# The last tail tile turned into token order and stored as plain rows, two late VectorE steps on ScalarE, and a new order of the last four pairs

## The chip, the cores and the metric

The kernel runs on one core of one Trainium2 chip. The metric is the device time of one execution in microseconds (us), from 3 runs; lower is better. A core has five engines with a queue each, which work side by side and wait for one another through semaphores: TensorE (PE: matrix products, with weight loads listed as PEld), VectorE (DVE), ScalarE (ACT), GpSimd (POOL) and SyncE (SP, used here to issue DMAs). ScalarE's queue issues a few DMAs too (ACTq in the profile). 16 DMA engines move the data.

## The reference

Attention with a relative position bias over 8 batches, 8 heads, 576 tokens and 64 values a head, and then a mixture of 8 rank-16 adapters on the 4608 rows of 512 columns that attention gives:

```python
scores = scale * np.matmul(q, k.transpose(0, 1, 3, 2)) + bias.transpose(2, 0, 1)[None, :, :, :]
attn = np.exp(scores - np.max(scores, axis=-1, keepdims=True))
attn = attn / (np.sum(attn, axis=-1, keepdims=True) + 1e-09)
x = (attn @ v).transpose(0, 2, 1, 3).reshape(B * S, H * D)
...
logits = x @ w_gate
topk = np.argpartition(-logits, K, axis=1)[:, :K]          # K = 2
w = np.exp(sel)                                             # the two logits, less the larger
w /= w.sum(-1, keepdims=True) + 1e-09
...
        z = x[mask] @ A[e]                                  # rows that chose adapter e in place k
        delta[mask] += w[mask, k, None] * (z @ B[e])
return (x + delta).astype(np.float32)
```

The bias depends on the distance of two tokens alone and is constant from distance 128 on.

## The kernel before

The work goes in 32 units, called pairs here: batch b and a pair of heads hp, `u = 4*b + hp`. The 576 tokens of a batch are 512 main tokens and a tail of 64. Main tokens are held in a strided order: partition p and block c hold token 4p + c, so a tile of 128 rows t (0 to 3) is the tokens 4p + t. Tails are held in the same manner, 16c + p for token 4p + c, and the tails of two batches share one tile of 128 rows (`xe`): batch 6 in rows 0 to 63, batch 7 in rows 64 to 127.

Each pair has the steps that one letter or two name in a table (`ORDER`, line 41), and `step` (line 838) carries them out. The table writes by hand the order in which every engine gets its instructions; an engine takes them in that order, and nothing reorders them later. The steps that matter here:

- `K0` to `K3`: scores of four blocks of keys on TensorE, then the exponential on ScalarE (lines 409 to 428; in the last pair `keys_part`, line 385, where K0 and K1 make the first half of the queries, K2 and K3 the second). The score tiles rotate through 3 buffers.
- `E`, `C`: edge and corner scores of the tails. `T`, `t`: transposes for a later pair and their copies on VectorE.
- `A`, `B` and `a`, `b`: products with the values on TensorE, and their normalisation on VectorE, both for the pair before.
- `Z z G W w V y D d S`: the adapters of a finished batch: gate logits and low-rank products, their gating on GpSimd and ScalarE, transposes, the product with `B` (`D`, a tile `dl`), the addition of x (`d`, `moe_add`, line 597) and the store (`S`). For the last two tiles of batch 6, x is added by four identity products on TensorE (line 805), and ScalarE copies the result.
- `l*`, `c*`: loads (issued on SP) and casts (on GpSimd).

In the last pair come the steps of the last group, the five tiles of batch 7 and the shared tail, in three parts: part 0 is tiles 0 and 1, part 1 tiles 2 and 3, part 2 tile 4 (the tail). `F01` and `F2` transpose the columns of the first three head pairs ahead of time (`last_x`, line 668); then `va`/`vb` (values), `norm`, `turn` and `copy` (transposes of the last columns and their copy), `za`/`zb` (logits and low-rank products), `ga` (top two, mask, tanh), `gb` (weights), `gt`/`gc` (transpose and copy), `delta` (product with `B`, line 801), `out` (output copy or addition) and `store`, each with its part or tile number and, at the end, the letter of its engine. Tile 4's output (`fol`) is stored in two halves, one from SP and one from ScalarE, in the form 4x16x512, four blocks of 16 rows: it brings the rows back into token order on the way to memory (`store_tail`, line 613). All output rows are 512 floats, 2 KB.

PSUM buffers: the pool `mm` has two that rotate among products, transposes and adapter tiles; at the end the banks of the scores become single tiles (`banks`, line 42).

Of the kernel before, what the change touches and what calls it, by code (L numbers as in the profile page):

```python
# [12 lines left out]
BF16 = mybir.dt.bfloat16  # L13
ALU = mybir.AluOpType
ACT = mybir.ActivationFunctionType
# [16 lines left out]
def _dram(t, offset, dims):  # L32
# [30 lines left out]
 'fin': '',  # L63
# [18 lines left out]
def kernel(  # L82
# [11 lines left out]
    nc = tc.nc  # L94
    B, H, S, D = q.shape
    NB = bias_table.shape[0]
    Dm = H * D
    E = moe_w_gate.shape[1]
    r = moe_A.shape[2]
    ER = E * r  # L100
    ZW = ER + E
    HP = H // 2
    scale = 1.0 / float(np.sqrt(D))
    inv = float(np.sqrt(D))
    FAR = 128
    SM = 512
# [7 lines left out]
    cp = ctx.enter_context(tc.tile_pool(name="const", bufs=1))  # L114
# [17 lines left out]
    half = [slice(0, 64), slice(64, 128)]  # L132
# [95 lines left out]
    for o in range(2):  # L228
        nc.vector.tensor_scalar(ones[NB * o:NB * o + NB, :GL - 33], bk[:, 32 * o:32 * o + GL - 33], row, None,
                                op0=ALU.is_equal)  # L230
    ident = cp.tile([128, 128], BF16, tag="ident")
# [48 lines left out]
    def select():  # L280
        nc.gpsimd.memset(sel, 0.0)
        nc.gpsimd.affine_select(out=sel, in_=sel, compare_op=ALU.not_equal, fill=1.0, base=-4,
                                pattern=[[1, 4 + Dm]], channel_multiplier=-4)

    AW = cp.tile([128, 4, ZW], BF16, tag="AW")
    Bc = cp.tile([ER, Dm], BF16, tag="Bc")
    A4f = cp.tile([128, E, 4, r], FP32, tag="A4f")
# [1 line left out]
    Bf = cp.tile([ER, Dm], FP32, tag="Bf")  # L289
    A4 = cp.tile([128, 4, ZW], BF16, tag="A4")  # L290
    sel = cp.tile([128, 4 + Dm], BF16, tag="sel")

    def weights_load():
        nc.sync.dma_start(out=A4f.rearrange("p e c r -> p e (c r)"),
# [296 lines left out]

    def moe_d(gr, t):
        dl = mp.tile([128, Dm], FP32, name="dl", tag="mm")
        delta(dl, gr.zT[t], gr.xT[t] if gr.last and t >= 2 else None)
        pending_d.append((gr, t, dl))

    def moe_add():
        gr, t, dl = pending_d.pop(0)
        ot = ms.tile([128, Dm], FP32, name="ot", tag="ot", bufs=4)
        if gr.last and t >= 2:  # L600
            nc.scalar.copy(ot, dl)
        else:
            nc.vector.tensor_tensor(ot, dl, gr.x[t], op=ALU.add)  # L603
        pending_s.append((gr, t, ot))
# [5 lines left out]
    def store_main(b, t, ot, eng=nc.sync):  # L610
        eng.dma_start(out=out[b * S:b * S + SM, :].rearrange("(p c) n -> p c n", c=4)[:, t, :], in_=ot)

    def store_tail(b, ot, engs=(nc.sync, nc.sync)):
        for o in range(2):
            engs[o].dma_start(out=out[(b + o) * S + SM:(b + o + 1) * S, :].rearrange("(p c) n -> c p n", c=4),
                              in_=ot[64 * o:64 * o + 64, :])


# [46 lines left out]
    fxs = cp.tile([128, HP * 640], BF16, tag="fx")  # L665
    fx = [fxs[:, i * 640:(i + 1) * 640].rearrange("p (n t) -> p n t", n=5) for i in range(HP)]

    def last_x(hps):
        x = [xs[B - 1][:, t, :] for t in range(4)] + [xe[(B - 1) // 2]]
        if len(hps) == 1:  # L670
            ps = mp.tile([128, 512], FP32, name="fx_ps", tag="mm")[:, :320]
        else:
            ps = score_tile("fx")[:, :, :320]
        for i, hp in enumerate(hps):
            w = (ps if len(hps) == 1 else ps[:, i, :]).bitcast(BF16).rearrange("p (n t) -> p n t", n=5)
            for t in range(5):
                nc.tensor.transpose(w[:, t, :], x[t][:, hp * 128:(hp + 1) * 128], ident)
        nc.vector.tensor_copy(fxs[:, hps[0] * 640:hps[0] * 640 + len(hps) * 640].rearrange("p (n t) -> p n t", n=len(hps)),
                              ps.bitcast(BF16) if len(hps) > 1 else ps.bitcast(BF16).rearrange("p (n t) -> p n t", n=1))

    fps = []

# [62 lines left out]
    def f_turn(g):  # L745
        w = take(f"t{g}")[:, :64 * len(parts[g])].bitcast(BF16).rearrange("p (n t) -> p n t", t=128)
        for i, t in enumerate(parts[g]):
            nc.tensor.transpose(w[:, i, :], x[t][:, xo:], ident)
        ps[f"t{g}"] = w

    def copier(eng):
# [12 lines left out]
                nc.tensor.matmul(fz[g]["z"][:, i, :], lhsT=fx[c][:, t, :], rhs=AW[:, c, :],  # L764
                                 start=(i == 0 and c == 0), stop=(c == 3), skip_group_check=True)

    def f_gate_a(g):
        l, n, z = fz[g], len(parts[g]), fz[g]["z"]
        top, ns, l["th"], l["mk"] = small(g, "top", 8), small(g, "ns", 1), small(g, "th"), small(g, "mk")
        for i in range(n):  # L770
            nc.vector.max(top[:, i, :], z[:, i, ER:])
        nc.vector.scalar_tensor_tensor(out=ns, in0=top[:, :, 0:1], scalar=-1.0,
                                       in1=top[:, :, 1:2], op0=ALU.mult, op1=ALU.subtract)
        nc.vector.tensor_tensor(l["mk"], z[:, :, ER:], top[:, :, 1:2].to_broadcast((128, n, E)),
                                op=ALU.is_ge)
        for i in range(n):
            nc.scalar.activation(l["th"][:, i, :], z[:, i, ER:], ACT.Tanh, scale=2.0, bias=ns[:, i, :])

    def f_gate_b(g):
        l, n, z = fz[g], len(parts[g]), fz[g]["z"]  # L780
        gate = small(g, "gate")
        nc.vector.scalar_tensor_tensor(out=gate, in0=l["th"], scalar=1.0, in1=l["mk"], op0=ALU.add,
                                       op1=ALU.mult)
        l["zt"] = ms.tile([128, n, E, r], BF16, name="fzt", tag=f"fzt{g}")
        nc.vector.scalar_tensor_tensor(out=l["zt"],
                                       in0=z[:, :, :ER].rearrange("p n (e r) -> p n e r", e=E),
                                       scalar=0.5, in1=gate.to_broadcast((128, n, E, r)),
                                       op0=ALU.mult, op1=ALU.mult)

    def f_gate_t(g):  # L790
# [10 lines left out]
    def delta(dl, zT, xT=None):  # L801
        nc.tensor.matmul(dl, lhsT=zT, rhs=Bc, start=True, stop=xT is None, skip_group_check=True)  # L802
        if xT is not None:
            for c in range(4):
                nc.tensor.matmul(dl[:, c * 128:(c + 1) * 128], lhsT=xT(c), rhs=ident,
                                 start=False, stop=(c == 3), skip_group_check=True)
# [4 lines left out]

    def f_out(t, eng):
        if t == 4:
            fz["ol"] = ms.tile([128, Dm], FP32, name="fol", tag="fol")
            o = fz["ol"]
        else:
            o = fot[t // 2][:, t % 2, :]
        if eng == "a":
            nc.scalar.copy(o, ps[f"d{t}"])
        else:  # L820
            nc.vector.tensor_tensor(o, ps[f"d{t}"], x[t], op=ALU.add)

    def f_store(t, eng):
        if t == 4:
            store_tail(B - 2, fz["ol"], (nc.sync, nc.scalar))
        else:
            engs[eng].dma_start(out=rows4[:, t, :], in_=fot[t // 2][:, t % 2, :])

# [155 lines left out]
```

## Time and profile before

| | |
|---|---|
| median of 3 runs | 193.26 us (193.12 to 193.83) |
| profiled execution | 191.99 us |
| its span, first to last instruction | 190.2 us |
| TensorE busy | 175.5 us (92%) |
| ScalarE busy | 162.2 us (85%) |
| VectorE busy | 142.7 us (75%) |
| GpSimd busy | 95.4 us (50%) |
| DMA | 39.25 MB, mean 206 GB/s |

Times within a profile are counted from the start of its span. Busy time is the sum of an engine's instructions; TensorE's ends are modelled, so its figure is no measure of how near its peak it is. In rows of a timeline the columns are start, duration, engine, line, operation, what is written and read, its count, and in brackets the idle time before it with what ended it.

### The profile page before, as it was taken

The page shows a single profiled execution, that of the slowest core. Times are in us where ns is not written, and L with a number is a line of the kernel's source. Part 1 is how long each engine was busy: PE and PEld are TensorE (multiplying, and loading weights), DVE is VectorE, ACT ScalarE, POOL GpSimd, SP SyncE. Part 2 cuts the span into 40 slices and gives each one's busy share as a digit, 9 for nine tenths or more (in the row PEclk, how much of TensorE's full clock was granted, in tenths as well). Part 3 has the DMA queues.
Part 4 walks back from the last instruction along what each step waited for, and adds up shares of the span by engine and source line. Part 5 has one row for each costly group of instructions (what it writes and reads, how often), then busy time and mean ns, then how long its engine had stood idle before and what let it go on. Part 6 is the DMA issues. An engine that isn't in the chain of part 4 may idle for free.

```text
span 190.2 us, 9407 instructions
## 1 busy us (share of the span) xinstructions
PE 175.5 (92%) x4028; PEld 124.8 (66%) x4028; DVE 142.7 (75%) x436; ACT 162.2 (85%) x192; POOL 95.4 (50%) x220
## 2 busy tenths in 40 slices
PE   6489999999999999999999999999999999999830
PEld 2245767787578777786678766876778667679510
DVE  4665666786788887889798788889788879777930
ACT  3089999989999999999998999999999999897620
POOL 7456838516961379336921597527703780720000
PEclk9999999999999999999999999999999999999996
DMA  4998799987978896989488997789697931113444
GB/s 159 237 267 240 205 252 275 295 179 199 274 230 184 263 257 188 248 246 276 126 241 175 299 264 229 182 264 262 161 245 174 319 109 59 59 59 104 163 143 146
DMA packets 71193, 39.25 MB, mean 206 GB/s; under 512 B 49520, under 2 KB 66416, under 8 KB 71152
## 3 DMA queue, kind: packets, MB, share of 16 engines
q1 hardware_dynamic: 70548, 37.96, 73.1%
q8 instruction: 31, 0.51, 1.2%
q10 hardware_dynamic: 604, 0.70, 1.1%
q14 instruction: 10, 0.08, 0.1%
HBM read 28.85 MB, written 9.44 MB: 201 GB/s over the span
## 4 chain that ended last, share of the span: by engine, by line
PE 70%; DMA 10%; SPq 6%; POOL 4%; ACT 2%; DVE 2%; issue 2%; ACTq 0%; POOLq 0%
PE sc L418 14%; PE pv L456 14%; PE tx L323 6%; PE sc L423 6%; PE dl L802 4%; DMA vs<-in_v_dram 4%; PE zl L536 4%; PE pv L475 4%; PE se L445 4%; DMA qkt<-in_k_dram 3%; PE pv L465 3%; SPq L153 3%; DMA A4f<-in_moe_A_dram 3%; SPq L156 2%; PE se L436 2%
## 5 line engine op out<-in xcount | busy, mean ns | idle before, releaser
L428 ACT ACTIVATE pk<-sc 128x1024 bf16<-128x1024 f32 x124 | 120.1, 1034 | 12.8 <-PE sc L423 12.6
L418 PE MATMUL sc<-qkT 64*64 64x512 bf16 x496 | 48.3, 397 | 1.6 <-DVE qkT L355 1.3
L456 PE MATMUL pv<-v,pk 128*128 128x65 bf16 x992 | 42.1, 194 | 0.0
L456 PEld LDWEIGHTS <-pk 128*128 128x128 bf16 x1024 | 38.1, 98 | 5.2 <-issue 3.5
L423 PE MATMUL sc<-Wt,anti 64*64 64x320 bf16 (+2 forms) x496 | 37.4, 279 | 0.1
L451 ACT ACTIVATE pt<-se 128x1024 bf16<-128x1024 f32 x32 | 33.4, 1045 | 1.8 <-PE se L447 0.9
L418 PEld LDWEIGHTS <-qkT 64*64 64x64 bf16 x496 | 15.8, 105 | 19.0 <-issue 5.4
L510 DVE TENSOR_TENSOR xn<-pv,rc 128x256 bf16<-128x256 f32 x62 | 26.3, 425 | 2.1
L360 DVE COPY qkT<-tx 128x512 bf16<-128x512 bf16 x32 | 22.0, 688 | 4.4 <-PE tx L323 3.9
L178 POOL CAST v<-vs 128x512 bf16<-128x512 f32 x32 | 19.8, 619 | 5.5 <-PE pv L456 2.8
L355 DVE COPY qkT<-tx 128x512 bf16<-128x512 bf16 (+2 forms) x32 | 21.5, 672 | 0.0
L603 DVE TENSOR_TENSOR ot<-dl,xn 128x512 f32<-128x512 f32 x26 | 17.5, 686 | 3.7 <-PE dl L802 3.7
L182 POOL CAST kn<-ks 128x512 bf16<-128x512 f32 x30 | 18.2, 611 | 3.2 <-DMA ks<-in_k_dram 3.0
L182 POOL CAST qn<-qs 128x512 bf16<-128x512 f32 x30 | 18.3, 610 | 1.8 <-DMA qs<-in_q_dram 1.5
L190 POOL CAST qkb<-qkt 128x512 bf16<-128x512 f32 x8 | 4.9, 611 | 27.9 <-DMA qkt<-in_k_dram 27.9
L509 DVE RECIPROCAL rc<-pv 128x4 f32<-128x4 f32 (+1 forms) x62 | 11.4, 184 | 9.2 <-PE pv L475 6.7
L465 PE MATMUL pv<-vc,pt 128*128 128x130 bf16 x124 | 17.0, 219 | 0.0
L423 PEld LDWEIGHTS <-anti 64*64 64x64 bf16 x496 | 15.6, 108 | 0.8 <-issue 0.6
L479 DVE TENSOR_TENSOR xe<-pv,rc 64x64 bf16<-64x64 f32 x62 | 13.6, 219 | 0.6
L547 DVE COPY z<-zl 128x272 f32<-128x272 f32 (+1 forms) x17 | 7.0, 414 | 7.9 <-PE zl L536 7.9
L445 PE MATMUL se<-qkT,tl 128*128 128x256 bf16 x64 | 12.8, 282 | 0.0
L323 PEld LDWEIGHTS <-kn 64*128 64x128 bf16 x256 | 6.0, 96 | 9.8 <-issue 3.4
(140 smaller groups left out, 293.2 us busy)
## 6 DMA issues: line engine op xcount, KB each, us to landing
qs<-in_q_dram SPq DMA_DIRECT2D x32, 256.0 KB, 3.3
vs<-in_v_dram SPq DMA_DIRECT2D x64, 128.0 KB, 4.7
ks<-in_k_dram SPq DMA_DIRECT2D x31, 256.0 KB, 4.1
out_dram<-ot SPq DMA_DIRECT2D x28, 256.0 KB, 5.5
qkt<-in_q_dram SPq DMA_DIRECT2D x8, 128.0 KB, 4.2
vt<-in_v_dram SPq DMA_DIRECT2D x16, 64.0 KB, 4.1
qkt<-in_k_dram SPq DMA_DIRECT2D x8, 128.0 KB
out_dram<-ot SPq DMA_DIRECT2D x6, 128.0 KB
```

What stands on the lines that cost most here:

```text
L178: eng.tensor_copy(t[:, :, :, :D].rearrange("p c h d -> p h c d"), s)
L182: copy(t.rearrange("p c h d -> p h c d"), s)
L355: nc.vector.tensor_copy(sb[:, k0:k1].rearrange("p k (g i) -> p g k i", g=2), ps[:, :, k0 * 64:k1 * 64].rearrange("p g (k i) -> p g k i", i ...
L360: nc.vector.tensor_copy(sb[:, 0:4].rearrange("p k j -> p (k j)").rearrange("p (g i c) -> p g i c", g=2, c=4), ps[:, :, 0:256].rearrange("p ...
L418: nc.tensor.matmul(sc[prt, h, :], lhsT=key_half(tx, h, m), rhs=tx[rows, 4:8, :], start=True, stop=False, skip_group_check=True)
L423: nc.tensor.matmul(_ap(sc[prt, h, :], p0, [[128, 4], [1, p1 - p0]]), lhsT=turned(h), rhs=_ap(Wt[rows, hp, :], p0 - 16 * m + 32, [[GY, 4], ...
L428: nc.scalar.activation(pks[u][:, c, :, :], sc, ACT.Exp, scale=scale)
L445: nc.tensor.matmul(sc[:, j, 256:], lhsT=tl[:, 1, hp, :], rhs=tx[:, 4:8, half[j]], start=False, stop=False, skip_group_check=True)
L451: nc.scalar.activation(pts[u].rearrange("p j (g h i) -> p h (j g) i", g=4, h=2), sc.rearrange("p h (g i) -> p h g i", g=8), ACT.Exp, scale ...
L456: nc.tensor.matmul(pv[:, o + h * W1:o + (h + 1) * W1], lhsT=pks[u][:, c, h, t * 128:(t + 1) * 128], rhs=vts[u % NV][:, c, h, :], start=(fi ...
L465: nc.tensor.matmul(pv[:, t * 2 * W1:(t + 1) * 2 * W1], lhsT=pts[u][:, 1, o:o + 128], rhs=tcs[b % 2][:, hp, :], start=False, stop=False, sk ...
L510: nc.vector.tensor_tensor(_ap(xs[b], 2 * x * Dm + hp * 128, [[Dm, 2], [D, 2], [1, D]]), _ap(pv, 0, [[2 * W1, 2], [W1, 2], [1, D]]), _ap(rc ...
```

## The change

- Tile 4's columns are transposed against a permuted identity (`inorder`) in `last_x` and `turn`, so that what comes out is in token order; its output then is stored as 64 plain rows a half. The new constant is made on GpSimd with `sel` in pair 1. The stores of the other tails stay as they were.
- The copy behind `F2` goes from VectorE to ScalarE, and so does tile 1's output in batch 6, with x added by identity products.
- `ns` is the sum of the top two logits and no longer its negative; signs further on turn with it.
- The table's rows for pairs 28 to 31 are new. Before, the last group's parts are gated in the order 0, 2, 1, and now 0, 1, 2.

```diff
@@ ORDER, pairs -4 to -1 (all four are new; one shown)
- -2: 'K1 t K0 K3 A B V L a cv S E y V y D w b K2 T',
+ -2: 'K1 K0 K3 D B d V cv K2 y d z E V b T t A y a',
@@ select
+        nc.gpsimd.memset(inorder, 0.0)
+        nc.gpsimd.affine_select(out=inorder, in_=inorder, compare_op=ALU.not_equal, fill=1.0, base=0,
+                                pattern=[[-64, 2], [-1, 16], [-16, 4]], channel_multiplier=1)
@@ moe_d
-        delta(dl, gr.zT[t], gr.xT[t] if gr.last and t >= 2 else None)
+        delta(dl, gr.zT[t], gr.xT[t] if gr.last and t >= 1 else None)
@@ moe_add
-        if gr.last and t >= 2:
+        if gr.last and t >= 1:
             nc.scalar.copy(ot, dl)
@@ last_x
-                nc.tensor.transpose(w[:, t, :], x[t][:, hp * 128:(hp + 1) * 128], ident)
-        nc.vector.tensor_copy(...)
+                nc.tensor.transpose(w[:, t, :], x[t][:, hp * 128:(hp + 1) * 128], ident if t < 4 else inorder)
+        if len(hps) == 1:
+            nc.scalar.copy(fxs[:, hps[0] * 640:hps[0] * 640 + 640], ps.bitcast(BF16))
+        else:
+            nc.vector.tensor_copy(...)
@@ f_turn
-            nc.tensor.transpose(w[:, i, :], x[t][:, xo:], ident)
+            nc.tensor.transpose(w[:, i, :], x[t][:, xo:], ident if t < 4 else inorder)
@@ f_gate_a, f_gate_b
-        nc.vector.scalar_tensor_tensor(out=ns, in0=top[:, :, 0:1], scalar=-1.0,
-                                       in1=top[:, :, 1:2], op0=ALU.mult, op1=ALU.subtract)
+        if eng == "p":
+            nc.gpsimd.tensor_tensor(ns, top[:, :, 0:1], top[:, :, 1:2], op=ALU.add)
+        else:
+            nc.vector.tensor_tensor(ns, top[:, :, 0:1], top[:, :, 1:2], op=ALU.add)
-            nc.scalar.activation(l["th"][:, i, :], z[:, i, ER:], ACT.Tanh, scale=2.0, bias=ns[:, i, :])
+            nc.scalar.activation(l["th"][:, i, :], z[:, i, ER:], ACT.Tanh, scale=-2.0, bias=ns[:, i, :])
-        nc.vector.scalar_tensor_tensor(out=gate, in0=l["th"], scalar=1.0, in1=l["mk"], op0=ALU.add,
+        nc.vector.scalar_tensor_tensor(out=gate, in0=l["th"], scalar=1.0, in1=l["mk"], op0=ALU.subtract,
-                                       scalar=0.5, in1=gate.to_broadcast((128, n, E, r)),
+                                       scalar=-0.5, in1=gate.to_broadcast((128, n, E, r)),
@@ f_store
-            store_tail(B - 2, fz["ol"], (nc.sync, nc.scalar))
+            for o in range(2):
+                (engs[eng], nc.scalar)[o].dma_start(out=out[(B - 2 + o) * S + SM:(B - 1 + o) * S, :],
+                                                    in_=fz["ol"][half[o], :])
```

The table has no step that asks for the GpSimd form of `ns`. Three places of the new order follow, with the rows of each engine as they stand in its queue (line, operation, written and read; x and a number for equal rows in a run). Lines are those of each file.

ScalarE, from behind the last pair's exponentials on, before:

```order
L755 COPY fxs<-f_5899 128x128
L777 ACTIVATE fth<-f_5901,fns 128x8 x2
L601 COPY ot<-dl 128x512 x2
L799 COPY fzT<-fm 128x256
L777 ACTIVATE fth<-f_5913,fns 128x8
L777 ACTIVATE fth<-f_5933,fns 128x8 x2
L819 COPY fot<-f_5971 128x512
L819 COPY fol<-f_6014 128x512
L615 DMA out_dram<-fol 4x16x512
L819 COPY fot<-f_6024 128x512
L827 DMA out_dram<-fot 128x512
```

and now:

```order
L684 COPY fxs<-fx_ps 128x640
L763 COPY fxs<-f_5872 128x128
L787 ACTIVATE fth<-f_5903,fns 128x8 x2
L606 COPY ot<-dl 128x512 x2
L809 COPY fzT<-fm 128x256
L787 ACTIVATE fth<-f_5946,fns 128x8 x2
L787 ACTIVATE fth<-f_5910,fns 128x8
L606 COPY ot<-dl 128x512
L830 COPY fot<-f_5992 128x512
L830 COPY fot<-f_6022 128x512
L840 DMA out_dram<-fot 128x512
L830 COPY fol<-f_6036 128x512
```

The copy of 640 columns (`fx_ps`) and a third copy `ot` are new on ScalarE; the tanh of tile 4 (one of 128x8) stands behind that of tiles 2 and 3; tile 3's output and its store stand ahead of tile 4's output (`fol`), whose half store, `out_dram` from `fol` 64x512, is ScalarE's last row behind these.

VectorE, from the last group's last max to its end (`ftop` to `fmk` are step `ga`, `fgate` and `fzt` are `gb`, `fzT` is `gc`, `fot` is `out`), before:

```order
L771 MAX ftop<-f_5933 128x8 x2
L772 SCALAR_TENSOR_TENSOR fns<-ftop 128x2
L774 TENSOR_TENSOR fmk<-f_5933,ftop 128x16
L782 SCALAR_TENSOR_TENSOR fgate<-fth,fmk 128x8
L785 SCALAR_TENSOR_TENSOR fzt<-f_5913,fgate 128x128
L782 SCALAR_TENSOR_TENSOR fgate<-fth,fmk 128x16
L785 SCALAR_TENSOR_TENSOR fzt<-f_5933,fgate 128x256
L799 COPY fzT<-fm 128x128
L821 TENSOR_TENSOR fot<-f_6007,xn 128x512
L799 COPY fzT<-fm 128x256
L821 TENSOR_TENSOR fot<-f_6030,xn 128x512
```

and now:

```order
L779 MAX ftop<-f_5910 128x8
L783 TENSOR_TENSOR fns<-ftop 128x1
L784 TENSOR_TENSOR fmk<-f_5910,ftop 128x8
L792 SCALAR_TENSOR_TENSOR fgate<-fth,fmk 128x16
L795 SCALAR_TENSOR_TENSOR fzt<-f_5946,fgate 128x256
L792 SCALAR_TENSOR_TENSOR fgate<-fth,fmk 128x8
L795 SCALAR_TENSOR_TENSOR fzt<-f_5910,fgate 128x128
L809 COPY fzT<-fm 128x256
L832 TENSOR_TENSOR fot<-f_6008,xn 128x512
L809 COPY fzT<-fm 128x128
L832 TENSOR_TENSOR fot<-f_6016,xn 128x512
```

Tile 4's rows (128x1, 128x8, 128x128) now stand behind those of tiles 2 and 3, and the copy of tiles 2 and 3 (`fzT`, 128x256) stands ahead of the addition `fot` and no longer behind it.

SP, its last stores, before:

```order
L611 DMA out_dram<-ot 128x512 x4
L615 DMA out_dram<-ot 4x16x512 x2
L611 DMA out_dram<-ot 128x512 x4
L827 DMA out_dram<-fot 128x512 x2
L615 DMA out_dram<-fol 4x16x512
L827 DMA out_dram<-fot 128x512
```

and now:

```order
L616 DMA out_dram<-ot 128x512 x3
L620 DMA out_dram<-ot 4x16x512 x2
L616 DMA out_dram<-ot 128x512 x4
L840 DMA out_dram<-fot 128x512 x3
L837 DMA out_dram<-fol 64x512
```

The half of the last tail goes last and has the form 64x512. The second row is the shared tail of batches 4 and 5.

More of the change, by code (lines that the diff above doesn't have):

```diff
@@ L291 @@
     sel = cp.tile([128, 4 + Dm], BF16, tag="sel")
+    inorder = cp.tile([128, 128], BF16, tag="inorder")
     def weights_load():
@@ L611, in store_main, with store_tail @@
         eng.dma_start(out=out[b * S:b * S + SM, :].rearrange("(p c) n -> p c n", c=4)[:, t, :], in_=ot)
-    def store_tail(b, ot, engs=(nc.sync, nc.sync)):
+    def store_tail(b, ot):
         for o in range(2):
-            engs[o].dma_start(out=out[(b + o) * S + SM:(b + o + 1) * S, :].rearrange("(p c) n -> c p n", c=4),
+            nc.sync.dma_start(out=out[(b + o) * S + SM:(b + o + 1) * S, :].rearrange("(p c) n -> c p n", c=4),
                               in_=ot[64 * o:64 * o + 64, :])
@@ L676, in last_x @@
             for t in range(5):
-                nc.tensor.transpose(w[:, t, :], x[t][:, hp * 128:(hp + 1) * 128], ident)
-        nc.vector.tensor_copy(fxs[:, hps[0] * 640:hps[0] * 640 + len(hps) * 640].rearrange("p (n t) -> p n t", n=len(hps)),
-                              ps.bitcast(BF16) if len(hps) > 1 else ps.bitcast(BF16).rearrange("p (n t) -> p n t", n=1))
+                nc.tensor.transpose(w[:, t, :], x[t][:, hp * 128:(hp + 1) * 128], ident if t < 4 else inorder)
+        if len(hps) == 1:
+            nc.scalar.copy(fxs[:, hps[0] * 640:hps[0] * 640 + 640], ps.bitcast(BF16))
+        else:
+            nc.vector.tensor_copy(fxs[:, hps[0] * 640:hps[0] * 640 + len(hps) * 640].rearrange("p (n t) -> p n t", n=len(hps)),
+                                  ps.bitcast(BF16))
     fps = []
@@ L765, in f_z, with f_gate_a @@
                                  start=(i == 0 and c == 0), stop=(c == 3), skip_group_check=True)
-    def f_gate_a(g):
+    def f_gate_a(g, eng=None):
         l, n, z = fz[g], len(parts[g]), fz[g]["z"]
@@ L813, in f_out @@
         if t == 4:
+            assert eng == "a"
             fz["ol"] = ms.tile([128, Dm], FP32, name="fol", tag="fol")
```

12 rows, old and new, of the table ORDER are left out of this document.

## The prediction

> **What bounds the kernel now.** I read the stretches of the span first (busy time of each engine by window, then granted clock, DMA share and GB/s), then the timeline of the last 20 us, then the chain of work that ended last. The rows below give, for each stretch: length, TensorE busy, weight loads, VectorE, ScalarE, GpSimd, clock, DMA share, GB/s.
>
> ```profile
> 165.00:170.00 5.00, 4.86 (x110) 3.54 (x109) 3.52 (x13) 4.57 (x6) 2.36 (x4) 1.00 0.28 108
> 170.00:175.00 5.00, 5.00 (x136) 4.45 (x129) 3.99 (x13) 4.35 (x5) 0.00 (x0) 1.00 0.32 79
> 175.00:180.00 5.00, 4.54 (x64) 3.33 (x62) 4.69 (x23) 2.75 (x10) 0.00 (x0) 1.00 0.33 124
> ```
>
> Until about 175 us TensorE is the bound: 5.00 us busy out of 5.00, with ScalarE next (4.35 to 4.57). After 175 us it isn't: the last group's gating is a chain that crosses TensorE, VectorE and ScalarE, and VectorE (4.69) is the busiest. After that only stores are left:
>
> ```profile
> 181.62 0.58 ACT L819 COPY fol<-f 128x512 f32<-128x512 f32 x1 [0.90 <-PE f L805]
> ...
> 182.23 0.55 SPq L615 DMA_DIRECT2D out_dram<-fol  x1
> 182.24 0.60 ACTq L615 DMA_DIRECT2D out_dram<-fol  x1
> ...
> 182.88 0.59 ACT L819 COPY fot<-f 128x512 f32<-128x512 f32 x1 [0.67 <-PE f L802]
> 183.35 0.34 SPq L827 DMA_DIRECT2D out_dram<-fot  x1
> 183.50 0.37 ACTq L827 DMA_DIRECT2D out_dram<-fot  x1
> ```
>
> The last store is issued at 183.50, yet the span ends at 190.2: 6.7 us in which no engine computes. The next rows say why. They are DMA windows around stores of the same 256 KB, quiet stretches first:
>
> ```profile
> 164.62 2.07 SPq L611 DMA_DIRECT2D out_dram<-ot  x2
> 170.56 1.25 SPq L615 DMA_DIRECT2D out_dram<-ot  x2
> ```
> ```profile
> 165.40:166.15 0.75, 0.75 (x24) 0.37 (x16) 0.75 (x2) 0.52 (x2) 0.75 (x1) 1.00 0.87 339
> ...
> 171.60:173.60 2.00, 2.00 (x60) 1.73 (x57) 1.31 (x6) 1.35 (x3) 0.00 (x0) 1.00 0.26 57
> ...
> 178.70:180.90 2.20, 1.46 (x12) 0.61 (x11) 1.97 (x13) 1.91 (x6) 0.00 (x0) 1.00 0.96 358
> 183.48:185.40 1.92, 0.00 (x0) 0.00 (x0) 0.00 (x0) 0.00 (x0) 0.00 (x0) 1.00 0.27 45
> 185.40:187.08 1.68, 0.00 (x0) 0.00 (x0) 0.00 (x0) 0.00 (x0) 0.00 (x0) 0.85 0.93 306
> 187.08:188.76 1.68, 0.00 (x0) 0.00 (x0) 0.00 (x0) 0.00 (x0) 0.00 (x0) 0.50 0.29 109
> 188.76:190.20 1.44, 0.00 (x0) 0.00 (x0) 0.00 (x0) 0.00 (x0) 0.00 (x0) 0.50 0.00 0
> ```
>
> A row store (L611, 128 rows) issued at 164.62 moves its data from 165.4 to 166.15: about 0.8 us from issue to data, 0.75 us of data at 339 GB/s, nearly all 16 DMA engines busy; three in a row keep 358 GB/s (178.70 to 180.90). A tail store (L615, two halves in the form 4x16x512) issued at 170.56 moves 57 GB/s with a DMA share of 0.26, about 4 of the 16 engines. The same picture stands at the very end: the halves of the last tail, issued at 182.23, run at share 0.27 and 45 GB/s until 185.4, the two row stores of 183.35 and 183.50 only get going then, and a narrow rest (share 0.29, 109 GB/s) lasts until 188.76. From the last byte to the end of the span are 1.44 us. So **the narrow tail store bounds the last 5 us.**
>
> **The change part by part.**
>
> *The store form.* Tokens of the last tail come out of the transposes in row order, so each half is stored as 64 rows, and no longer as 4x16x512. The DMA count and the bytes stay. The trace shows no 64-row store of this kind. The fast end for both halves together is the row store, 262 KB in 0.73 us (358 GB/s); the slow end is the tail store itself, 1.92 us at 45 GB/s and the rest at 109. I take the fast end: the narrow form differs from the row store in that four blocks stand outermost, and about four engines work; what replaces it has 64 rows outermost, like the row store's 128. The tail of batches 4 and 5 (170.56) keeps the old form; its addition and with it the store come some 3 us earlier, under TensorE's work, at no cost.
> The Trainium skill bears on this: "DMA: Bandwidth & Descriptors", section "Why a DMA increments its semaphore by 16 and not by 1", says that the hardware path takes the largest number up to 16 that divides the slowest dimension of both access patterns, here 4 before and 16 after. The shares of 0.26 and 0.27 agree for the old form; no run yet shows the new one. By that rule the time would be the forecast's 189.7; if the form made no difference, it would be the 192.5 of the first rival.
>
> *The order at the end.* Before, tile 4 (the tail) goes through the gate ahead of tiles 2 and 3; now tiles 2 and 3 go first and tile 4, half as wide, last. Up to the last values' products TensorE has the same instructions in the last two pairs apart from order, and it is the bound there, so those products end near 175.7 in both. From there I walk the new order with the old rows:
>
> ```profile
> 176.43 0.42 DVE L735 TENSOR_TENSOR xn<-f,frc 128x256 bf16<-128x256 f32 x1
> ...
> 177.20 0.68 DVE L603 TENSOR_TENSOR ot<-dl,xn 128x512 f32<-128x512 f32 x1
> ...
> 177.72 0.58 ACT L601 COPY ot<-dl 128x512 f32<-128x512 f32 x1
> 177.74 0.28 PE L748 MATMUL f<-ident,xn 128*128 128x128 bf16 x2
> ...
> 178.07 0.42 DVE L785 SCALAR_TENSOR_TENSOR fzt<-f,fgate 128x256 bf16<-128x256 f32 x1
> ...
> 178.41 0.28 DVE L755 COPY fxs<-f 128x256 bf16<-128x256 bf16 x1
> ...
> 179.08 0.25 DVE L771 MAX8 ftop<-f 128x8 f32<-128x8 f32 x2
> ...
> 180.36 0.42 DVE L785 SCALAR_TENSOR_TENSOR fzt<-f,fgate 128x256 bf16<-128x256 f32 x1
> ...
> 180.84 0.68 DVE L821 TENSOR_TENSOR fot<-f,xn 128x512 f32<-128x512 f32 x1
> ...
> 181.43 0.28 DVE L799 COPY fzT<-fm 128x256 bf16<-128x256 bf16 x1
> ```
>
> The second normalisation (L735) keeps its place within 0.1 us: VectorE loses one copy ahead of it (0.48, below) and gets an addition of 0.68 there that it used to do earlier. The turn of tiles 2 and 3 (PE L748, 177.74) stood behind products that now follow it; it comes at about 177.0, and its copy (178.41) at 177.3. VectorE finishes the gate of tiles 0 and 1 (178.07 + 0.42) at 178.4 to 178.5 as before, and can then start the max of tiles 2 and 3 at once: 178.4 for 179.08, 0.7 earlier. Tanh and weighting keep that lead (180.36 becomes 179.7). The copy of their transposed result (181.43) gains 0.3 more, since the addition of 0.68 that stood ahead of it now stands behind it: about 180.45. So tile 3's output copy on ScalarE moves from 182.88 to about 181.6, and ends at 182.2. Tile 4 follows: the addition 0.68 delays its copy on VectorE to 181.65, 0.21 for the copy, 0.45 for its products and the identity's, and its output copy can run on ScalarE from 182.45, behind tile 3's store issue (0.37), to 183.05. The last issue then is at 183.05 for 183.50. I take 183.2, 0.3 earlier, because such a walk is good to some 0.15 us a step; bounds: 0.9 earlier, and 0.6 later.
>
> *VectorE steps on ScalarE.* The copy of the third block of columns and the addition of tile 1 of the group before:
>
> ```profile
> L678 DVE COPY fxs<-fx_ps 128x640 bf16<-128x640 bf16 x1 | 0.5, 480 | 0.0
> ...
> L799 ACT COPY fzT<-fm 128x256 bf16<-128x256 bf16 x1 | 0.4, 378 | 0.0
> ```
> ```profile
> 176.11 0.27 ACT L755 COPY fxs<-f 128x128 bf16<-128x128 bf16 x1 [0.86 <-PE f L748]
> ...
> 177.10 0.39 PE L805 MATMUL dl<-ident,qkT 128*128 128x128 bf16 x4
> ```
>
> VectorE loses 0.48 + 0.68 us. ScalarE gets a copy of 640 columns, which I put at 0.70 us (0.27 for 128 columns and 0.378 for 256 make 0.11 per 128), and one of 0.58; TensorE gets four identity products (0.39). ScalarE's idle time covers them: 5.00 - 2.75 = 2.25 us in 175 to 180. They are inside the walk above; uncovered, they would cost 0.70 + 0.58 = 1.28.
>
> *The permuted identity.* One memset and one select on GpSimd in pair 1, 128x128 like the identity's own:
>
> ```profile
> 1.37 0.19 POOL masks.py:197 MEMSET ident<- 128x128 bf16 x1
> 1.64 0.29 POOL masks.py:199 TENSOR_SCALAR_AFFINE_SELECT ident<-ident 128x128 bf16<-128x128 bf16 x1
> ...
> 24.25 0.61 POOL L182 CAST qn<-qs 128x512 bf16<-128x512 f32 x1
> ...
> 28.38 0.61 POOL L301 CAST A<-A4f 128x512 bf16<-128x512 f32 x1 [2.85 <-DMA A4f<-in_moe_A_dram]
> ```
> ```profile
> 25.39 0.29 PE L323 MATMUL tx<-ident,kn 64*128 64x64 bf16 x8 [0.37 <-ACT pk L428]
> ```
>
> That is 0.19 + 0.29 = 0.48 us ahead of four casts on an in-order queue. The cast of 24.25 would end at 25.34, and the transposes that need it ran at 25.39, held by ScalarE. Then GpSimd waits 2.85 us for a load, which swallows the delay. I take 0 (bounds 0 and 0.48).
>
> *Gate arithmetic and pairs 28 to 31.* The sum in place of one fused VectorE step and the changed signs keep instruction counts. The new order of the pairs moves the same products; with TensorE and ScalarE at 4.86 and 4.57 of 5.00 there is little to win and something to lose, 0 with bounds of 0.3 either way.
>
> **The sum.** Row stores of tile 3 and tile 2 go out at 182.2 and 182.6, the tail's halves at 183.2. First data 0.8 later, at 183.0; three times 0.73 us of data end at 185.2, for 188.76 before. With the same 1.44 us the span ends at 186.65, for 190.2: 3.55 less. The profiled execution took 191.99 us for its span of 190.2, and the runs have a median of 193.26; taken off that, 189.7.
>
> **The rivals.**
> 1. *The new form stays narrow* (the change doesn't do what it says). For it: no row shows a 64-row store. Against it: the share of a quarter fits the four outermost blocks. Then from 183.2: 1.25 us to the first data (182.23 to about 183.48), 1.92 us at 45 GB/s (86 KB), the other 176 KB at 109 GB/s 1.6 us, so 188.0, plus 1.44 is 189.4: 0.8 less, 192.5.
> 2. *ScalarE becomes the bound at the end*, because both moved steps land ahead of copies that the chain needs. For it: its copies stand in one queue with tanh. Against it: 2.25 us idle. All 1.28 us on the chain: last issue 184.5, span 187.9, time 191.0.
> 3. *The rows' place in memory, not the number of engines, makes the tail store slow*, so that plain neighbouring rows are slow through and through. For it: four engines alone reach 109 GB/s at share 0.29, so the 45 GB/s at 0.27 needs another cause as well. Against it: row stores write to such rows at 358 GB/s. At 45 GB/s for all 262 KB (5.8 us): 183.2 + 1.25 + 5.8 + 1.44 = 191.7, 1.5 more than 190.2, so 194.8. It decides from 60 GB/s down: there the tail costs 4.4 us of data and the gain is all but gone.
>
> **How the numbers follow.** 0.79 for the forecast (188.6 to 190.5 by itself: the bounds of the walk, 0.5 for GpSimd at the upper end, and the runs' own spread of 0.7), 0.09 for rival 2, 0.08 for rival 1, 0.04 for rival 3. The range takes in the forecast and rival 2 with some room: 188.6 to 191.4. Half a per cent, about what a measurement of this kernel can tell from no change, is 0.97 us: forecast and rival 2 are faster by more (0.88), rival 1 lies within (0.08), rival 3 is slower (0.04).
>
> **What would show it.** Right: in the last windows the DMA share stays near 0.9 from the first of the last stores to the last byte, with no stretch at 0.27; the last byte comes about 2 us after the last issue; the issue of a half takes about 0.35 us and no longer 0.55 to 0.60. Tiles 2 and 3 have their max near 178.4 and the last issue is near 183.2. Wrong: a share of a quarter after the last issue (rivals 1 and 3, told apart by GB/s), ScalarE without gaps from 176 us on with TensorE waiting for its copies (rival 2), or VectorE's last products later than 175.7.

## The result and the profile after

| | before | changed |
|---|---|---|
| median of 4 runs | 193.51 us (193.12 to 193.83) | 190.65 us (189.97 to 191.01) |
| ratio | | 0.9849, 95% interval 0.9813 to 0.9885 |
| profiled execution, its span | 191.99, 190.2 us | 190.5, 188.7 us |

The change takes 2.86 us off, between 2.2 and 3.6 by the interval; 189.7 was predicted, with a range of 188.6 to 191.4.

The two profiled spans differ by 1.5 us only, and a comparison of them by the clock would mislead, so this comes first. The windows of the same stretch in both kernels (before, then after; length, TensorE, weight loads, VectorE, ScalarE, GpSimd, clock, DMA share, GB/s):

```profile
20.00:60.00 40.00, 38.98 (x943) 28.40 (x941) 29.40 (x87) 37.87 (x43) 23.94 (x48) 1.00 0.91 232
```
```profile
20.00:60.00 40.00, 37.49 (x909) 27.25 (x903) 28.09 (x83) 36.69 (x41) 24.90 (x50) 1.00 0.87 226
```

In this execution of the changed kernel TensorE did 1.49 us less work between 20 and 60 us, far ahead of the last pairs. How late the same place in the program comes varied over the kernel before, the changed one and all the kernels that follow, by up to 4 us (153.40 to 157.39), with the same code in front of it but for the making of the new constant. So times here are counted from **the mark**: the start of ScalarE's edge exponential of pair 28, the first pair with a new order. Step `E` of pair 27 issues it, so it stands just ahead of the new rows of the table. In the timelines of before and of after:

```profile
153.40 1.04 ACT L451 ACTIVATE pt<-se 128x1024 bf16<-128x1024 f32 x1
```
```profile
154.99 1.04 ACT L456 ACTIVATE pt<-se 128x1024 bf16<-128x1024 f32 x1
```

From the mark to the end of the span it is 190.2 - 153.40 = 36.80 us before and 188.7 - 154.99 = 33.71 after, **3.09 less**; the profiles now tell what the timed runs tell. Rows of after are 1.59 us late against rows of before for a reason that is not in the last pairs; take that off to compare.

The timeline of after, for the rows of the end that the prediction walked through:

```profile
176.31 0.69 ACT L684 COPY fxs<-fx_ps 128x640 bf16<-128x640 bf16 x1 [0.23 <-PE fx_ps L682]
...
177.78 0.42 DVE L743 TENSOR_TENSOR xn<-f,frc 128x256 bf16<-128x256 f32 x1
...
178.28 0.27 PE L756 MATMUL f<-ident,xn 128*128 128x128 bf16 x2
...
178.66 0.29 DVE L763 COPY fxs<-f 128x256 bf16<-128x256 bf16 x1
...
179.74 0.24 DVE L779 MAX8 ftop<-f 128x8 f32<-128x8 f32 x2
...
181.15 0.42 DVE L795 SCALAR_TENSOR_TENSOR fzt<-f,fgate 128x256 bf16<-128x256 f32 x1
...
181.96 0.29 DVE L809 COPY fzT<-fm 128x256 bf16<-128x256 bf16 x1
...
183.17 0.59 ACT L830 COPY fot<-f 128x512 f32<-128x512 f32 x1 [1.14 <-PE f L815]
...
184.81 0.54 SPq L837 DMA_DIRECT2D out_dram<-fol  x1
184.81 0.57 ACTq L837 DMA_DIRECT2D out_dram<-fol  x1
```

And the windows of after around the last issue at 184.81:

```profile
175.00:180.00 5.00, 4.64 (x85) 4.04 (x83) 4.53 (x18) 3.21 (x8) 0.00 (x0) 1.00 0.15 57
...
184.70:186.20 1.50, 0.00 (x0) 0.00 (x0) 0.00 (x0) 0.08 (x1) 0.00 (x0) 0.96 1.03 363
186.20:186.80 0.60, 0.00 (x0) 0.00 (x0) 0.00 (x0) 0.00 (x0) 0.00 (x0) 0.50 0.93 215
186.80:187.15 0.35, 0.00 (x0) 0.00 (x0) 0.00 (x0) 0.00 (x0) 0.00 (x0) 0.50 0.76 287
187.15:188.70 1.55, 0.00 (x0) 0.00 (x0) 0.00 (x0) 0.00 (x0) 0.00 (x0) 0.50 0.00 0
```

Where 0.27 and 0.29 stood as the share of the DMA engines, 1.03, 0.93 and 0.76 stand now. The last issue comes 29.82 us after the mark (30.10 before), and 3.89 us lie between it and the end (6.70 before). So 2.81 of the 3.09 us came out of the time after the last issue and 0.28 out of the work ahead of it. What is not as predicted is the stretch at 215 GB/s: the engines are busy there, but bytes move at little over half of 363.

### The profile page after: what moved, and what is told of

It reads as the page before. It is cut to its first block, busy times and chain, and to the rows that moved or that the text cites. A ratio compares the mean times of both kernels' runs of the same rounds, so it can differ in the third digit from the quotient of the medians.

```text
span 188.7 us, 9418 instructions
## 1 busy us (share of the span) xinstructions
PE 175.3 (93%) x4032; PEld 125.0 (66%) x4032; DVE 142.1 (75%) x434; ACT 163.2 (86%) x194; POOL 96.2 (51%) x222
## 4 chain that ended last, share of the span: by engine, by line
PE 68%; DMA 9%; SPq 8%; ACT 4%; DVE 3%; POOL 3%; issue 3%; ACTq 0%; POOLq 0%
PE sc L423 15%; PE pv L461 14%; PE tx L328 6%; PE sc L428 6%; DMA vs<-in_v_dram 4%; PE se L450 4%; PE zl L541 4%; PE dl L812 4%; PE pv L480 4%; DMA ks<-in_k_dram 3%; PE pv L470 3%; SPq L153 2%; PE se L441 2%; SPq L156 2%; ACT pk L408 2%
## 5 line engine op out<-in xcount | busy, mean ns | idle before, releaser
L608 DVE TENSOR_TENSOR ot<-dl,xn 128x512 f32<-128x512 f32 x25 | 16.8, 686 | 3.7 <-PE dl L812 3.1
```

## The experiments

Every kernel is compared by two numbers of its profile: mark to end (before 36.80, after 33.71), and the last store issue, counted from the mark (30.10, 29.82). Ratios to the kernel before are given where runs were timed. Where a result is from a single profiled run, the spread of mark to end between kernels with the same end can serve as a measure: before and build_only have 36.80 both, after, identity_late and sixteen_blocks 33.71, 33.66 and 33.69.

### The store form alone, and everything but the store form

store_only is the kernel before, in its old order, with the permuted identity and the plain rows:

```diff
@@ last_x, f_turn
-  ident)
+  ident if t < 4 else inorder)
@@ f_store
-            store_tail(B - 2, fz["ol"], (nc.sync, nc.scalar))
+            for o in range(2):
+                (engs[eng], nc.scalar)[o].dma_start(out=out[(B - 2 + o) * S + SM:(B - 1 + o) * S, :],
+                                                    in_=fz["ol"][half[o], :])
```

> The kernel before, with the permuted identity and the 64-row stores of the last tail alone; order of the pairs, order of the last group and the VectorE steps as before. Theory 1 (the narrow form of the store delays the end): the last store is still issued at about 183.5 us, but the last byte comes some 2.2 us later and not 5.3, so 3.0 us less than before: 190.5 us, ratio 0.984 to 0.986. Theory 2 (the new order at the end and the ScalarE steps bring the gain): same as before, 193.5, ratio 0.998 to 1.002.

narrow_store is the changed kernel with the old form of that store and the plain identity for tile 4:

```diff
-  out=out[(B - 2 + o) * S + SM:(B - 1 + o) * S, :],
+  out=out[(B - 2 + o) * S + SM:(B - 1 + o) * S, :].rearrange("(p c) n -> c p n", c=4),
```

> The changed kernel with its last tail stored as before, in the form 4x16x512, and the plain identity. Theory 1: the DMA share falls to a quarter after the last issue, last byte about 5 us after it; 192.5 to 193.3 us, ratio 0.995 to 0.999. Theory 2: the gain stays, 190.7, ratio 0.985.

Measured: store_only 191.46 us (6 runs), ratio 0.9878 (0.9842 to 0.9914), mark to end 34.44, last issue 30.07. That is theory 1, but with 2.4 us of the 3.0 it named. narrow_store 193.61 us (12 runs), ratio 0.9997 (0.9970 to 1.0025), mark to end 36.69, last issue 29.80: theory 1 again, at a little more than its 193.3. The windows of narrow_store, whose halves are issued at 184.91:

```profile
184.90:186.10 1.20, 0.00 (x0) 0.00 (x0) 0.00 (x0) 0.00 (x0) 0.00 (x0) 0.76 1.04 370
186.10:187.00 0.90, 0.00 (x0) 0.00 (x0) 0.00 (x0) 0.00 (x0) 0.00 (x0) 0.50 0.43 73
187.00:188.70 1.70, 0.00 (x0) 0.00 (x0) 0.00 (x0) 0.00 (x0) 0.00 (x0) 0.50 0.19 59
188.70:190.25 1.55, 0.00 (x0) 0.00 (x0) 0.00 (x0) 0.00 (x0) 0.00 (x0) 0.50 0.22 85
```

As soon as the row stores are through (370 GB/s), the halves are alone, at a share of 0.19 to 0.43 and 59 to 85 GB/s for over 4 us. With the old form nearly the whole gain is gone, in spite of the new order in front of it: the new order alone is worth 36.80 - 36.69 = 0.11 us. The form alone is worth 36.80 - 34.44 = 2.36 us in the old order, and 36.69 - 33.71 = 2.98 in the new one. The rest of the total, 0.73, is what the new order gives once the form is wide. The windows of store_only, whose halves are issued at 185.11, ahead of the last two row stores (186.23 and 186.33):

```profile
186.30:187.00 0.70, 0.00 (x0) 0.00 (x0) 0.00 (x0) 0.00 (x0) 0.00 (x0) 0.79 0.94 187
187.00:188.80 1.80, 0.00 (x0) 0.00 (x0) 0.00 (x0) 0.00 (x0) 0.00 (x0) 0.50 0.97 363
188.80:190.70 1.90, 0.00 (x0) 0.00 (x0) 0.00 (x0) 0.00 (x0) 0.00 (x0) 0.50 0.00 0
```

Against the changed kernel 0.25 of the 0.73 lies ahead of the last issue (30.07 for 29.82), some 0.1 between it and the last byte (188.80 - 186.33 = 2.47 for 2.34), and 0.35 behind the last byte (1.90 for 1.55). So the bytes explain little of it; why the time behind the last byte is longer there, no run shows.

### Blocks outermost or place in memory

Two things were changed at once by the form: how many blocks stand outermost, and which rows of memory follow one another. sixteen_blocks keeps the store out of order but with 16 blocks of 4 rows outermost (the rows of the tail land in another order than the reference has); four_plain keeps neighbouring rows but with 4 blocks outermost, of 15 rows (4 of the 64 rows of a half are left out, and the others land in another order):

```diff
@@ sixteen_blocks
-  out=out[(B - 2 + o) * S + SM:(B - 1 + o) * S, :],
+  out=out[(B - 2 + o) * S + SM:(B - 1 + o) * S, :].rearrange("(c p) n -> p c n", c=4),
@@ four_plain
+  out=out[...].rearrange("(c p) n -> c p n", c=4)[:, :15, :], in_=fz["ol"][64 * o:64 * o + 60, :]
```

> The changed kernel with each half of the last tail stored in the form 16x4x512 (16 blocks of 4 rows that lie 16 rows apart), so the rows land in another order. Measured from the start of the exponential of pair 28's edges to the end of the span, which came out at 36.80 us for the kernel before and 33.71 for the changed one. Theory 1a (the number of blocks outermost sets how many DMA engines work, and that is what cost the time): 33.6 to 34.0, share near 0.9 after the last issue. Theory 1b (the rows' places in memory: a store that takes rows out of their order is slow): 35.5 or more, share about a quarter.

> The changed kernel with each half of the last tail stored as 4x15x512, four blocks of 15 neighbouring rows; 4 of 64 rows a half are left out, and the others land in another order. Same interval. Theory 1a: about four engines again, 36.0 to 36.7. Theory 1b: neighbouring rows go fast, 33.5 to 34.0.

Measured: sixteen_blocks 190.23 us (4 runs), ratio 0.9825 (0.9778 to 0.9872), mark to end 33.69. four_plain 193.36 us (10 runs), ratio 0.9975 (0.9940 to 1.0011), mark to end 36.26. Both lie where theory 1a put them. The last windows of the one and of the other, after issues at 184.41 and 183.94:

```profile
184.40:185.70 1.30, 0.00 (x0) 0.00 (x0) 0.00 (x0) 0.00 (x0) 0.00 (x0) 1.00 1.01 367
185.70:186.70 1.00, 0.00 (x0) 0.00 (x0) 0.00 (x0) 0.00 (x0) 0.00 (x0) 1.00 0.81 264
```
```profile
183.90:185.20 1.30, 0.00 (x0) 0.00 (x0) 0.00 (x0) 0.01 (x1) 0.00 (x0) 1.00 1.02 366
185.20:186.60 1.40, 0.00 (x0) 0.00 (x0) 0.00 (x0) 0.00 (x0) 0.00 (x0) 0.91 0.29 70
186.60:188.80 2.20, 0.00 (x0) 0.00 (x0) 0.00 (x0) 0.00 (x0) 0.00 (x0) 0.50 0.21 74
```

Scattered rows in 16 blocks are fast, neighbouring rows in 4 blocks are slow, at a share of 0.21 to 0.29 and 70 to 74 GB/s, although four_plain writes 1/16 fewer bytes. So the number of outermost blocks decides, and the place in memory doesn't. The rule of the Trainium skill that the prediction weighed ("DMA: Bandwidth & Descriptors", "Why a DMA increments its semaphore by 16 and not by 1") has held in both directions: the largest number up to 16 that divides the slowest dimension of both patterns is 4 in four_plain (60 and 4) and 16 in sixteen_blocks (64 and 16). The shares agree: 0.21 to 0.29 is about 4 of the 16 engines, and 0.81 takes 13 of them or more.

### What the permuted identity costs

build_only is the kernel before with the constant made in pair 1 and not used; identity_late is the changed kernel with the constant made behind pair 12:

```diff
@@ build_only: select
+        nc.gpsimd.memset(inorder, 0.0)
+        nc.gpsimd.affine_select(out=inorder, ...)
@@ identity_late: both lines into token_order(), and behind the steps of a pair
+        if u == 12:
+            token_order()
```

> The kernel before, with the permuted identity made in pair 1 and not used. Theory 3: 0.5 us slower than before, ratio 1.002 to 1.003. Theory 4: no difference, 0.999 to 1.001.

> The changed kernel with the permuted identity made on GpSimd at the end of pair 12 and not in pair 1. Theory 3 (the 0.48 us on GpSimd in pair 1 delay TensorE, which runs without gaps later, so that all of it is lost): 0.5 us less than the changed kernel, ratio 0.982 to 0.983, and TensorE's idle time up to 60 us falls by as much. Theory 4 (GpSimd's wait for a load swallows it, and TensorE's idle time up to 60 us differs from execution to execution by itself): as the changed kernel, 0.985.

Measured: build_only 193.44 us (12 runs), ratio 0.9983 (0.9956 to 1.0009), mark to end 36.80. identity_late 190.77 us (6 runs), ratio 0.9822 (0.9776 to 0.9868), mark to end 33.66. The interval of build_only reaches from 0.85 us less to 0.17 more, so there is no cost to see, and theory 3's 0.5 us lies outside it. Mark to end can't show such a cost, since pair 1 lies ahead of the mark. identity_late decides nothing by its time: its interval holds what both theories named. But its mark is at 155.44 without the constant in pair 1, so a late mark like the changed kernel's (154.99) doesn't need the constant.

### The two steps on ScalarE

moves_back takes the copy behind `F2` and the addition of tile 1 back to VectorE, in the changed kernel:

```diff
@@ moe_d, moe_add
-  t >= 1
+  t >= 2
@@ last_x
-            nc.scalar.copy(fxs[:, hps[0] * 640:hps[0] * 640 + 640], ps.bitcast(BF16))
+            nc.vector.tensor_copy(fxs[:, hps[0] * 640:hps[0] * 640 + 640], ps.bitcast(BF16))
```

> The changed kernel with the copy behind F2 and the addition of tile 1 of batch 6 back on VectorE. Same interval. Theory 5 (VectorE is the bound of the last group, the walk of the prediction): the second normalisation comes 0.4 to 0.5 us later, tiles 2 and 3 follow, 34.1 to 34.3. Theory 6 (ScalarE's two extra copies hold the chain up): 33.3 to 33.5.

Measured: mark to end 34.55, last issue 30.70, 0.88 later than the changed kernel's (one run of 192.52 us beside 193.84 for the kernel before). The new place costs nothing that shows, and the old one 0.84 us: theory 5, and more than the 0.4 to 0.6 it named. The rows of moves_back tell how:

```profile
177.46 0.49 DVE L684 COPY fxs<-fx_ps 128x640 bf16<-128x640 bf16 x1
...
179.89 0.28 PE L756 MATMUL f<-ident,xn 128*128 128x128 bf16 x2
...
181.37 0.68 DVE L608 TENSOR_TENSOR ot<-dl,xn 128x512 f32<-128x512 f32 x1
...
181.97 0.24 DVE L779 MAX8 ftop<-f 128x8 f32<-128x8 f32 x2
```

Its mark is at 156.15. The turn of tiles 2 and 3 then comes 23.74 us after the mark, for 178.28 - 154.99 = 23.29 in the changed kernel: 0.45 of the copy's 0.49. The addition of 0.68 at 181.37 stands ahead of the max of tiles 2 and 3, which comes at 25.82 for 24.75: 1.07 late, of which the end keeps 0.84.

### The order of the pairs ahead of the last row

old_pairs is the changed kernel with the old rows for pairs 28 to 30 and a `d` ahead of the new last row, which the old rows leave to do.

```diff
- -4: 'ck K3 y cv D z d A lq ...'   -3: 'lq T d cq cv C lv ...'   -2: 'K1 K0 K3 D B d V ...'
+ -4: 'lv K2 y y S z d ck K0 ...'   -3: 'lv lk G K2 d y T ...'    -2: 'K1 t K0 K3 A B V ...'
- -1: 'B S K1 K0 b
+ -1: 'd B S K1 K0 b
```

> The changed kernel with the order of before for pairs 28 to 30 (and one step d at the start of the last pair, so that the addition that is pending there is done). Same interval. If the order of these pairs is worth nothing, as the prediction has it: 33.4 to 34.0. If it carries the 0.28 us by which the last issue came earlier: 34.0 or more with the last issue at 30.1 after the start mark.

Measured: mark to end 35.04, last issue 31.10 (one run of 191.78 us, beside 193.84 before), a full 1 us later than the 30.1 that the expectation named. The changed kernel's windows of that stretch, and then those of old_pairs, whose mark is at 154.96, only 0.03 away:

```profile
155.00:175.00 20.00, 19.96 (x482) 14.82 (x475) 15.74 (x48) 18.70 (x23) 7.40 (x20) 1.00 0.25 82
```
```profile
155.00:175.00 20.00, 18.95 (x453) 13.78 (x447) 14.60 (x44) 17.61 (x22) 7.29 (x20) 1.00 0.20 66
175.00:180.00 5.00, 4.95 (x101) 4.37 (x99) 4.51 (x17) 3.21 (x6) 0.00 (x0) 1.00 0.21 77
180.00:186.00 6.00, 4.06 (x39) 2.37 (x38) 4.19 (x18) 4.34 (x12) 0.00 (x0) 1.00 0.63 234
```

TensorE is busy 18.95 of 20 us in place of 19.96, and the last issue comes 1.28 us later, the end 1.33. So the new last row needs the new rows ahead of it. That isn't a gain of 1.3 us against the kernel before, whose rows fit together as well: the whole new order has its last issue 0.28 earlier only. Which of the moved steps makes TensorE wait in the mixture was not tried.

### What sets the end now

Three questions about the time behind the last issue. Do the bytes of the other stores hold the halves up? no_store2 leaves out the store of tile 2 of batch 7 (its rows are not written):

```diff
-  out.2.v store.3.a S out.4.a store.2.s S store.4.s L',
+  out.2.v store.3.a S out.4.a S store.4.s L',
```

> The changed kernel without the store of tile 2 of batch 7 (256 KB left out, its rows aren't written). Interval from the start of the exponential of pair 28's edges to the end of the span, 33.71 us for the changed kernel, with the last issue 29.82 after the mark. Theory 7 (the DMA engines are full from some 27.5 us after the mark to the last byte, so the bytes bound the end): 0.5 to 0.8 less, 32.9 to 33.2, with the last issue where it was. Theory 8 (a fixed time from the last issue to the last byte): 33.6 to 33.8.

Measured: mark to end 33.61, 0.10 less, and 3.82 us behind the last issue for 3.89. The other stores' bytes don't bound the end. With nothing beside them, the halves show their own pace, from their issue at 187.17 on:

```profile
188.25:189.05 0.80, 0.00 (x0) 0.00 (x0) 0.00 (x0) 0.00 (x0) 0.00 (x0) 0.50 0.81 164
189.05:189.45 0.40, 0.00 (x0) 0.00 (x0) 0.00 (x0) 0.00 (x0) 0.00 (x0) 0.50 0.88 328
```

First data 1.1 us behind the issue, then half speed at a share of 0.81, then nearly full speed. Both stretches move 131 KB, the size of one half. The DMA view by queue says whose they are, for 188.25 to 189.02 and then for 189.05 to 189.45 (queue, packets, MB, share; q1 carries what SP issues, q10 what ScalarE issues):

```profile
q1 hardware_dynamic: 63, 0.13, 82.4%
```
```profile
q10 hardware_dynamic: 75, 0.13, 84.4%
```

So the halves don't move side by side: SP's goes first, at 164 GB/s, and then ScalarE's, of the same form, at 328. Is the first one slow because two queues start at once? one_queue is no_store2 with both halves issued from SP:

```diff
-                (engs[eng], nc.scalar)[o].dma_start(...)
+                (engs[eng], engs[eng])[o].dma_start(...)
```

> The changed kernel without tile 2's last store (those rows are not written), and with both halves of the tail's store issued from SP, one behind the other, where SP and ScalarE issued one each at the same time. Disputed: why the halves' 262 KB take 1.25 us, the first 0.8 us of it at 138 to 174 GB/s with a DMA share of 0.63 to 0.93. Theory 9 (two queues that start at once slow each other): the first half then runs alone at over 280 GB/s, its 131 KB in about 0.45 us from 1.0 us after its issue, and the second half likewise, 0.55 later; last byte 2.0 to 2.1 us after the first half's issue. Theory 10 (64 rows on 64 partitions are slow by themselves): each half runs at 140 to 210 GB/s also when alone, 0.65 to 0.9 us for one; last byte 2.5 to 2.8 us after the first half's issue. From the mark (start of ScalarE's edge exponential of pair 28) to the end: theory 9 33.4 to 33.6, theory 10 33.9 to 34.2, against 33.61 with two queues.

Measured: mark to end 33.88. From the first issue at 186.42:

```profile
187.50:188.85 1.35, 0.00 (x0) 0.00 (x0) 0.00 (x0) 0.00 (x0) 0.00 (x0) 0.88 0.89 190
```

One behind the other the halves move 190 GB/s all along, with no fast part, at a share of 0.89: theory 9 (the two queues slow each other) falls. The pace is the one that theory 10 named; its last byte came 2.43 us after the first issue, just short of the 2.5 it named, and mark to end just short of its 33.9. But theory 10 (64 rows on 64 partitions are slow by themselves) doesn't hold either, since ScalarE's half in no_store2 moves at 328 GB/s, close to a store of 128 rows (339 to 358 GB/s). Nor is it SP's queue alone: in rows_first (below), where ScalarE's half is issued first, q10 is the slow one (187.00 to 187.30, 198 GB/s) and SP's half runs at 287 GB/s behind it (187.35 to 187.85):

```profile
q10 hardware_dynamic: 27, 0.06, 85.4%
```
```profile
q1 hardware_dynamic: 71, 0.12, 65.2%
```

With two queues the half that goes first is slow and the other one isn't; with one queue both are. Why is open. Two queues help: mark to end is 33.61 with them and 33.88 without.

Can the end be shortened by the order? shorter_end puts tile 3's store last, behind the halves, with its addition on VectorE (the expectation below names its other moves); rows_first puts it ahead of them:

```diff
@@ shorter_end, end of the last row
+ ... S store.1.s out.0.a store.0.s delta.2.v delta.3.v delta.4.a out.2.v store.2.s out.4.a store.4.s out.3.v store.3.s
@@ rows_first
+ ... S store.1.s out.0.a store.0.s delta.2.v delta.3.v delta.4.a out.2.v store.2.s out.3.v store.3.s out.4.a store.4.s
```

> The changed kernel with another order of the last steps: tile 4's transpose ahead of the products of tiles 2 and 3, its copy straight behind theirs on VectorE, tile 0 copied out by ScalarE (x added by identity products) and tile 3 by VectorE. By the changed kernel's rows the last issue comes at about 184.05 for 184.81, 0.7 earlier. Theory 7 (bytes bound the end): six stores of 0.73 us from 182.4 end at 186.8 for 187.15, interval 33.3 to 33.4. Theory 8: 33.0.

> As shorter_end, but tile 3's output and store stand ahead of the tail's halves on SP. Theory 11 (in shorter_end the row store lost because its issue stood behind the half's issue of 0.54 us, and its data behind the halves'): the row store goes out 28.9 to 29.1 us after the mark, the last half 29.4 to 29.5, and the span ends 33.2 to 33.5 us after the mark. Theory 12 (the end is set by when the bytes of the last three stores can move, whatever their order): 33.7 to 33.9, as in shorter_end (33.80) and the changed kernel (33.71).

Measured: shorter_end mark to end 33.80, with the last issue at 29.62 (one run of 190.24 us, beside 193.86 before); both of its expectations missed, since the last issue came 0.2 earlier and 4.18 us followed it. rows_first 33.55, last issue 29.45 (191.14 beside 193.49), a little over what theory 11 gave (33.2 to 33.5) and under theory 12. So the order explains a part of shorter_end's miss, 0.25 us: 0.17 at the last issue and 0.08 behind it. The windows of rows_first show why no more comes:

```profile
183.20:186.20 3.00, 0.98 (x7) 0.45 (x7) 1.44 (x3) 0.74 (x2) 0.00 (x0) 0.90 1.02 369
186.20:187.80 1.60, 0.00 (x0) 0.00 (x0) 0.00 (x0) 0.00 (x0) 0.00 (x0) 0.50 0.98 284
```

From 183.20 to the last byte the DMA engines have no gap any more: the stores' bytes, the last of them partly at the slow half's pace, now bound this version. Against the changed kernel it has 0.16 us less by the profile, but in one run, and that run's time (191.14) is above the changed kernel's median; it isn't shown to be faster. No version here beats the changed kernel by more than the runs can tell.

## Why the prediction was right, point by point

- **What bounds the end.** Right: the narrow store bounded the time behind the last issue, and it alone takes all but 0.11 us of the gain back (narrow_store). Its mechanism was the forecast's, four outermost blocks: four_plain and sixteen_blocks rule out rival 3 (the place in memory). The argument against that rival, that row stores write to such rows, was no test of it: a row store writes every fourth row of memory (`rows4`, line 702 before), as each block of the old form does, and not neighbouring rows. Rival 1 (the new form stays narrow) didn't come; as a price for the old form it was too kind, 192.5, where narrow_store has 193.61.
- **The walk along the last group's chain.** Right to 0.3 us at every row. Taking the 1.59 us off the changed kernel's rows: second normalisation at 176.2 (predicted to stay at 176.4 within 0.1), turn of tiles 2 and 3 at 176.7 (predicted 177.0), its copy 177.1 (177.3), max of tiles 2 and 3 178.15 (178.4), weighting 179.6 (179.7), transposed copy 180.4 (180.45), tile 3's output copy 181.6 (181.6), last issue 183.2 (183.2). The early rows are 0.1 to 0.3 us ahead of the forecast and that lead is gone at the output copy; so two small errors cancel, and that the last issue comes out to the tenth is luck.
- **VectorE steps on ScalarE.** Right that ScalarE's idle time covers them: the copy took 0.69 (predicted 0.70), ScalarE had 3.21 us busy of 5.00 from 175 to 180, and rival 2 (ScalarE becomes the bound) didn't come. What they bring VectorE stood inside the walk without a number; moves_back gives it, 0.84.
- **The permuted identity.** Right: 0, by build_only.
- **The pairs 28 to 31 at 0, within 0.3.** The sum fits (0.28 at the last issue, the walk included), but no run tells this term apart from the walk, and as a statement on a part it is wrong: the old rows with the new end lose 1.3 (old_pairs).
- **The time behind the last issue.** The mechanism right, one term mis-sized. The step "I take the fast end: the narrow form differs from the row store in that four blocks stand outermost" put the halves at 358 GB/s and 0.73 us. Alone they take 1.2 us (no_store2): the half that goes first needs 0.8, at half of that pace, and the other one 0.4. In the changed kernel, with 1.59 us taken off, the row stores are through at 184.6, near the sum's 183.0 + 2 x 0.73, and what is left of the halves then takes 0.95 us for 0.73. The last byte came 2.34 us after the last issue for 2.0, and then 1.55 to the end for 1.44: together 3.89 for 3.45. That is 0.44 of the 0.46 us by which the measured gain from the mark (3.09) falls short of the predicted one (3.55).
- **The issue of a half at 0.35 us.** Wrong: 0.54 and 0.57, as before the change (0.55 and 0.60). What the two forms share that makes them slow to issue was not tried. The sum didn't hang on it.

The other half of the distance from 189.7 to 190.65 is no step of the sum: the kernel before took 193.51 in the runs beside it, for the 193.26 that the sum started from, which makes 0.25, and the rest, some 0.25, lies within the spread of the runs (0.7 for the kernel before, 1.0 for the changed one).

## What to carry to other kernels

At a kernel's end, where nothing runs beside it, look at the DMA share of the last stores and not at their bytes: a store with 4 blocks outermost kept about a quarter of the engines busy, and the same bytes with 16 or 64 outermost were some 3 us faster, so it pays to put the reordering into a product that is there anyway, with a permuted identity in place of the plain one. With the row stores ahead of the halves the end came 0.25 us sooner here (rows_first against shorter_end), in one profile each. And compare two profiles from a common row just ahead of the change: the start of these kernels varied by more than the whole change was worth.

## What the runs showed of the hardware that was not expected

- Two stores of 64 rows of 2 KB, issued from SP and ScalarE at the same time, move one after the other, the first at 164 GB/s with a DMA share of 0.81 and the second at 328 with 0.88 (no_store2); both issued from SP, they run at 190 with 0.89 (one_queue). A store of 128 rows has 339 to 358 GB/s at a share of 0.87 to 0.96. A busy DMA engine isn't one at its full pace.
- Four blocks move 59 to 85 GB/s when alone (narrow_store), which is less than a quarter of 358; no single number for the form holds, as before the change it was 45 at first and 109 later.
- The issue of a half takes 0.54 to 0.59 us in the form of 64 rows and 0.55 to 0.62 in that of 4x16 (0.62 in narrow_store). In the last 12 us a store of 128 rows takes 0.33 to 0.38 (0.53 once, right behind a half, in shorter_end). So fewer rows took longer to issue.
- Between executions with the same code ahead of it, but for the making of one constant, the start of pair 28's edge exponential lay anywhere from 153.40 to 157.39 us.
